# A long convolution by FFT stages, then soft MoE slots: the first stage in three products of column halves, with other stores and loads around it

## The chip, the cores and the metric

The kernel runs on one core of one Trainium2 chip. All data is float32. The metric is the device time of one execution in microseconds; before the change it is 932.87 us, the median of three runs (930.76 to 934.02). A core has a matrix engine (TensorE, PE in the profile; its weight loads are PEld), VectorE (DVE), ScalarE (ACT), GpSimd (POOL) and SyncE (SP), which here only issues DMAs. Sixteen DMA engines move data between the chip's memory (HBM) and the on-chip SBUF. TensorE writes to PSUM, and ScalarE or VectorE carry its results from there to SBUF; that is called an eviction.

## The reference

```python
def _attn_ref(x, h):                 # x: (8, 5696, 128), h: (5696, 128)
    L = 2 * S
    Xf = np.fft.rfft(x, n=L, axis=1)
    Hf = np.fft.rfft(h, n=L, axis=0)
    return np.fft.irfft(Xf * Hf[None], n=L, axis=1)[:, :S, :]

def _moe_ref(x, phi, w1, w2):        # x: the result above as (45568, 128); 32 slots, 8 experts
    logits = x @ phi
    d = softmax of logits over the tokens
    slot_input = d.T @ x
    slot_out[e] = np.maximum(slot_input[e] @ w1[e], 0) @ w2[e]
    c = softmax of logits over the slots
    return c @ slot_out
```

Each of the 8 sequences is convolved causally with h along its 5696 positions, channel by channel. The result goes through a soft mixture of experts: every token is weighed into 32 slots, the slots pass through small networks, and each token gets a mixture of the slots back.

## The kernel before, in words

**The transform.** A sequence is seen as a table of R1 = 89 rows by N2 = 64 columns (a position is row times 64 plus column), padded in theory to N1 = 90 rows. A transform over the rows gives 90 frequencies k1; for each of these a transform over the 64 columns follows. Columns n and 63 - n are folded first: their sum and their difference are transformed separately with cosines and sines of half the size. That makes these stages:

- *Stage A* (`stage_a`, lines 204 to 219): for a chunk of CH = 4 columns of the lower half and the 4 mirrored ones, multiply the folded rows by a table over all 90 frequencies. For the sum (comp 0) the two products are the cosine table and the negative sine table; for the difference (comp 1) they are the negative sine table and the negative cosine table. Each product is one matmul of 128 rows by 128 table columns on 512 elements (4 columns of 128 channels). The 90 frequencies lie as two groups of 45 table columns, at F0 = 6 and F1 = 82. ScalarE evicts each product into a buffer `fst` (three of these), and two DMAs store it to a scratch tensor f in HBM, one for each group: 45 partitions, 4 columns, and runs of 1 KB (cosine and sine part of 128 channels). So a chunk costs four matmul products, four evictions and four stores of 180 KB.
- *Stage B1* (`stage_b1`): for two frequencies at a time (a "unit", 23 in a sequence), load f from HBM (`load_g`, line 230, tile gt, 256 KB in 128 partitions, 2 KB runs), transform over the columns, and multiply with the spectrum of h (Hr, Hi).
- *Stage B2* (`stage_b2`): the way back over the columns; evicted into `zst` (five buffers) and stored to a scratch tensor z in HBM (line 289, 256 KB, 1 KB runs).
- *Stages C1 to C6*: for two chunks at a time ("a pair T") load z (`load_pair`, line 319: 1024 KB and 416 KB, 16 KB runs), go back over the rows, unfold, transpose, and do the logits, both softmaxes and the sum into the slots, with a running maximum.

h is treated as sequence 0; its B1 makes Hr and Hi. After the last tokens the experts are computed and every token's output is made and stored.

**Loading x.** `load_x` (lines 178 to 191) fetches one chunk: for each of 89 rows, two runs of 2 KB, the lower columns and the mirrored ones. It does so in two DMAs, of 80 and of 9 rows, to partitions 20 to 108 of one of three buffers `xc`. The other partitions hold zeros, and so do those rows of the table. `fold` (lines 195 to 202) makes the sum or the difference on GpSimd, each into its own single buffer, `x0` or `x1`, of [128, 512].

**The order of the work.** The order is written out by hand: a loop over steps t (line 557), one chunk a step, with the stages of earlier data woven in at fixed lags (LAG_B = 9 steps, LAG_C = 27). Every engine takes its instructions in this order, and SyncE issues all loads and stores in this order too, one after the other; an issue whose buffer isn't free, or whose data isn't there, holds up all that follow. A step has about three units of B in its `slot_b` calls; each first loads gt for a unit four units ahead, unless that unit belongs to a new sequence whose f isn't complete. Every second step has the work of a pair (C1, C4, C5), the others its transposes and sums (C2, C3, dispatch).

In a step before the change the order is: stage A on the sum, with its stores; the fold of the next chunk's sum; dispatch; slot_b; C1, C4, C2, C6; slot_b; the load of a pair; the load of chunk t + 3; the additions of C1; C5; stage A on the difference, with its stores; the fold of the next difference; C3; slot_b; the rest of the softmaxes.

Steps 0 to 71 have stage A; after that the same loop goes on without it, until the last units are through.

Of the kernel before, what the change touches and what calls it, by code (L numbers as in the profile page):

```python
# [10 lines left out]
F32 = mybir.dt.float32  # L11
AF = mybir.ActivationFunctionType
# [10 lines left out]
def transform_tables(S, N1, N2, CH, X0, F0, F1):  # L23
# [21 lines left out]
    part = s1  # L45
    s1 = np.zeros((P, 3, P))
    for a, p in enumerate((F0, F1)):
        s1[X0:X0 + R1, :, p:p + NP] = part[:, :, a * NP:(a + 1) * NP]
# [26 lines left out]
def kernel(  # L75
# [42 lines left out]
    SPLIT = R1 // 16 * 16  # L118
    X0, F0, F1 = 20, 6, 82
# [4 lines left out]
        for n, t in zip(("s1", "i1", "w", "v", "turn"), transform_tables(S, N1, N2, CH, X0, F0, F1))]  # L124
# [35 lines left out]
    s1 = apool.tile([P, 3, P], F32, name="s1", tag="s1", bufs=1)  # L160
# [13 lines left out]
    xcs = [apool.tile([P, 2, CH, D], F32, name=f"xc{i}", tag=f"xc{i}", bufs=1) for i in range(3)]  # L174
# [3 lines left out]
    def load_x(c):  # L178
        if c >= (B + 1) * NJ:
            return  # L180
        g, j = divmod(c, NJ)
        src = (h if g == 0 else x[g - 1]).rearrange("(a n) d -> a n d", n=N2)
        t_ = xcs[c % len(xcs)]
        gap = N2 - CH * (2 * j + 1)
        for r in (slice(0, SPLIT), slice(SPLIT, R1)):
            v = src[r, CH * j:CH * (j + 1), :]
            v = bass.AP(tensor=v.tensor, offset=v.offset,
                        ap=[v.ap[0], [gap * D, 2], [1, CH * D]])
            nc.sync.dma_start(
                out=t_[X0 + r.start:X0 + r.stop, :, :, :].rearrange("p s n d -> p s (n d)"), in_=v)  # L190
        xs[c] = t_
# [3 lines left out]
    def fold(c, comp):  # L195
        if c not in xs:
            return
        t_ = xs.pop(c) if comp else xs[c]
        y_ = xf[comp]
        nc.gpsimd.tensor_tensor(out=y_[:, :, :], in0=t_[:, 0, :, :], in1=t_[:, 1, ::-1, :],  # L200
                                op=AL.subtract if comp else AL.add)
        folded[(c, comp)] = y_

    def stage_a(c, comp):
        g, j = divmod(c, NJ)
        src = folded.pop((c, comp))
        tab = (0, 1) if comp == 0 else (1, 2)
        st = apool.tile([P, CH, 2, D], F32, name="fst", tag="fst", bufs=3)
        for G in range(2):
            p = bank()  # L210
            nc.tensor.matmul(p[:, :], s1[:, tab[G], :],  # L211
                             src[:, :, :].rearrange("p n d -> p (n d)"), start=True, stop=True)
            nc.scalar.activation(st[:, :, G, :],  # L213
                                 p[:, :].rearrange("p (n d) -> p n d", d=D), AF.Copy)
        n0 = comp * HALF + CH * j
        for a, p in enumerate((F0, F1)):
            nc.sync.dma_start(
                out=fd[g][a, n0:n0 + CH, :, :, :].rearrange("n q c d -> q n (c d)"),
                in_=st[p:p + NP, :, :, :].rearrange("k n c d -> k n (c d)"))
# [54 lines left out]
    def stage_b2(u):  # L274
# [12 lines left out]
        st = bpool.tile([P, 2, 2 * D], F32, name="zst", tag="zst", bufs=5)  # L287
# [257 lines left out]
    nc.scalar.dma_start(out=s1[:, :, :], in_=t_s1)  # L545
    for c in range(1, 3):
        load_x(c)
# [9 lines left out]
    for t in range(last_front + 1):  # L557
# [83 lines left out]
        stage_a(t, 0)  # L641
        fold(t + 1, 0)
        if t == NA - 1:
            stage_a(t, 1)
        if pair(3) is not None:
            dispatch(pair(3))
        slot_b()
        T, U = pair(0), pair(2)
# [11 lines left out]
        slot_b()  # L660
        if pair(-2) is not None:
            load_pair(pair(-2))
        load_x(t + 3)
# [6 lines left out]
        if t < NA - 1:  # L670
            stage_a(t, 1)
            fold(t + 1, 1)
# [236 lines left out]
```

## Time and profile before

| | us | share of the span |
|---|---|---|
| span of the profiled run | 933.3 | |
| PE busy | 842.3 | 90% |
| DVE busy | 664.2 | 71% |
| ACT busy | 511.5 | 55% |
| POOL busy | 469.6 | 50% |
| L211, stage A's matmuls (576 instructions) | 284.3 | |
| L213, their evictions (288, 597 ns each) | 167.7 | |
| L200, the folds (144, 1277 ns each) | 183.7 | |
| L336, C1's matmuls in column halves (448 instructions) | 112.9 | |

A float32 matmul product appears as two instructions, so the 288 products of stage A are 576 entries. The DMA queue moves 273.04 MB in 172,239 packets, 293 GB/s on average.

A page of the profile gives each engine's busy time, and then its course over the span in 40 slices, where a digit 9 means 90% or more. A busy PE isn't PE at its peak, since matmuls are pipelined and their ends are modelled. The DMA share is the mean over sixteen engines, so it can hide that some carry less than others. In the waits, "A <- B" means that A sat idle until B let it go; for SyncE's queue, "SPq", an issue stood still.

The run falls into parts: up to some 100 us stage A and the spectrum of h, up to some 225 us stages A and B, from there to 690 us all stages together, and then the last sequence's B and C, the experts, and from about 850 us the output.

### The profile page before, as it was taken

What the parts mean: (1) busy time and instruction counts of PE and PEld (TensorE: products, weight loads), DVE (VectorE), ACT (ScalarE), POOL (GpSimd) and SP (SyncE); (2) the same over time, 40 slices, a digit from 0 to 9 for tenths busy, and PEclk for the clock granted to TensorE, in tenths of its full rate; (3) what the DMA queues carried; (4) which work ended last, traced back from release to release, by engine and by line L of the source; (5) the groups of instructions that cost most, each with busy time, mean ns of one, the idle gap of its engine ahead of it and who ended that gap; (6) DMA issues with size and microseconds to landing.
All of it is one profiled execution on the core that took longest, in us unless ns stands there. A gap on an engine that the chain in (4) does not pass through costs nothing. (4 is left out here: it accounts for less than half of the span.)

```text
span 933.3 us, 20359 instructions
## 1 busy us (share of the span) xinstructions
PE 842.3 (90%) x7220; PEld 402.3 (43%) x7220; DVE 664.2 (71%) x1127; ACT 511.5 (55%) x1016; POOL 469.6 (50%) x431
## 2 busy tenths in 40 slices
PE   6978788899999999999999999989998888996893
PEld 2323233334444444444444444434443434453793
DVE  3035576678878877888888788858878886795542
ACT  3556544455656655666666566646664444574442
POOL 4647623245555555555555555545545665468000
PEclk9989999999999999999999999989999988998956
DMA  9999899999999989999999999989979886675798
GB/s 296 272 270 277 264 325 316 295 306 318 284 296 311 332 262 298 321 328 279 291 308 333 280 310 309 308 270 307 319 258 279 288 269 230 218 273 196 272 405 327
DMA packets 172239, 273.04 MB, mean 293 GB/s; under 512 B 14742, under 2 KB 117398, under 8 KB 168965
## 3 DMA queue, kind: packets, MB, share of 16 engines
q1 hardware_dynamic: 171563, 271.38, 90.9%
q8 instruction: 58, 0.95, 0.4%
q10 hardware_dynamic: 576, 0.36, 0.2%
q14 instruction: 42, 0.34, 0.1%
HBM read 142.85 MB, written 128.21 MB: 290 GB/s over the span
## 5 line engine op out<-in xcount | busy, mean ns | idle before, releaser
L211 PE MATMUL bank<-x,s 128*128 128x512 f32 x576 | 284.3, 621 | 9.9 <-POOL x L200 8.0
L200 POOL TENSOR_TENSOR x<-xc 128x512 f32<-128x512 f32 x144 | 183.7, 1277 | 144.9 <-PE bank L211 90.8
L213 ACT ACTIVATE fst<-bank 128x512 f32<-128x512 f32 x288 | 167.7, 597 | 91.7 <-PE bank L211 63.6
L265 DVE TENSOR_TENSOR pr<-bt,Hr 128x512 f32<-128x512 f32 (+1 forms) x184 | 126.6, 688 | 100.1 <-PE bt L244 97.1
L288 ACT ACTIVATE zst<-bz 128x512 f32<-128x512 f32 (+1 forms) x184 | 108.2, 588 | 153.7 <-PE bz L284 147.8
L244 PE MATMUL bt<-gt,wt 64*64 64x256 f32 x1620 | 140.1, 409 | 45.8 <-DMA gt<-f 16.1
L211 PEld LDWEIGHTS bank<-x,s 128*128 128x128 f32 x576 | 100.1, 192 | 133.2 <-issue 88.8
L270 DVE TENSOR_TENSOR yf<-pr,pi 128x512 f32<-128x512 f32 (+1 forms) x169 | 145.2, 859 | 5.8
L268 DVE TENSOR_TENSOR pi<-bt,Hi 128x512 f32<-128x512 f32 (+1 forms) x184 | 125.0, 679 | 0.0
L284 PE MATMUL bz<-yf,vt 64*64 64x256 f32 x1440 | 118.7, 389 | 2.2 <-ACT yt L371 0.5
L244 PEld LDWEIGHTS bt<-gt,wt 64*64 64x64 f32 x1620 | 45.4, 133 | 163.1 <-PE bank L211 45.3
L336 PE MATMUL bank<-zc,i 128*64 128x512 f32 x448 | 112.9, 628 | 0.0
L359 POOL TENSOR_TENSOR y<-y,op 128x512 f32<-128x512 f32 x64 | 77.5, 1211 | 60.3 <-DVE op L341 57.7
L359 POOL TENSOR_TENSOR y<-y,om 128x512 f32<-128x512 f32 x54 | 75.9, 1405 | 2.1
L284 PEld LDWEIGHTS bz<-yf,vt 64*64 64x64 f32 x1440 | 53.2, 134 | 37.8 <-issue 12.8
L255 DVE SCALAR_TENSOR_TENSOR Hr<-bt,turn,ph 128x128 f32<-128x128 f32 (+1 forms) x46 | 16.0, 348 | 68.9 <-ACT ph L253 68.9
L371 ACT ACTIVATE yt<-bank 128x360 f32<-128x360 f32 x128 | 51.9, 472 | 15.8 <-PE bank L369 15.6
L369 PE MATMUL bank<-ident,y 109*128 109x109 f32 x512 | 58.9, 268 | 1.0 <-DVE y L359 0.7
L415 POOL MEMSET dt<- 64x8 f32 x32 | 3.4, 107 | 109.3 <-ACT dn L418 87.0
L369 PEld LDWEIGHTS bank<-ident,y 109*128 109x128 f32 x512 | 50.5, 145 | 16.6 <-issue 10.8
L860 PE MATMUL op<-so,cT 32*128 32x128 f32 x704 | 44.9, 376 | 6.2 <-ACT o L869 5.8
L336 PEld LDWEIGHTS bank<-zc,i 128*64 128x64 f32 x448 | 28.1, 140 | 51.4 <-issue 46.3
(100 smaller groups left out, 910.1 us busy)
## 6 DMA issues: line engine op xcount, KB each, us to landing
f<-fst SPq DMA_DIRECT2D x288, 180.0 KB
gt<-f SPq DMA_DIRECT2D x198, 256.0 KB
z<-zst SPq DMA_DIRECT2D x176, 256.0 KB
zc<-z SPq DMA_DIRECT2D x28, 1024.0 KB
xc<-in_x_dram SPq DMA_DIRECT2D x64, 320.0 KB
out_dram<-o SPq DMA_DIRECT2D x15, 1024.0 KB
zc<-z SPq DMA_DIRECT2D x28, 416.0 KB
out_dram<-o SPq DMA_DIRECT2D x9, 768.0 KB
```

The lines of the kernel that those rows point to most:

```text
L200: nc.gpsimd.tensor_tensor(out=y_[:, :, :], in0=t_[:, 0, :, :], in1=t_[:, 1, ::-1, :], op=AL.subtract if comp else AL.add)
L211: nc.tensor.matmul(p[:, :], s1[:, tab[G], :], src[:, :, :].rearrange("p n d -> p (n d)"), start=True, stop=True)
L213: nc.scalar.activation(st[:, :, G, :], p[:, :].rearrange("p (n d) -> p n d", d=D), AF.Copy)
L244: nc.tensor.matmul(bt[q * HP:(q + 1) * HP, a, 0:2 * D], wt[r, 2 * i + q, :], t_[r, q, :, :].rearrange("p c d -> p (c d)"), start=True, sto ...
L265: nc.vector.tensor_tensor(out=pr[r, :, :, :], in0=pv, in1=Hr[r, i, :, :].unsqueeze(2).broadcast_to([n * HP, 2, 2, D]), op=AL.mult)
L268: nc.vector.tensor_tensor(out=pi[r, :, :, :], in0=pv, in1=Hi[r, i, :, :, :], op=AL.mult)
L270: adder.tensor_tensor(out=y_[r, :, :, :], in0=pr[r, :, :, :], in1=pi[r, :, ::-1, :], op=AL.add)
L284: nc.tensor.matmul(bz[a * HP:(a + 1) * HP, q, 0:2 * D], vt[r, i, a, :], y_[r, a, :, :].rearrange("p c d -> p (c d)"), start=True, stop=True)
L288: nc.scalar.activation(st[:, 0:n, :], bz[:, 0:n, 0:2 * D], AF.Copy)
L336: nc.tensor.matmul(p[h_ * HP:(h_ + 1) * HP, :], i1[:, tab, :], t_[:, h_, o, :, q, :], start=True, stop=True)
L359: eng.tensor_tensor(out=part_, in0=part(v, 0), in1=o_[:, :, :], op=sign)
L369: nc.tensor.transpose(p[:, i * TR:(i + 1) * TR], ys[T][0:TR, k * CH + i, 0:D], ident[0:TR, 0:TR])
```

## The change

Four things change together.

1. *Three products.* Sum and difference of a chunk share one matmul product in PSUM: the sum's 64 table columns give partitions 0 to 63, the difference's give 64 to 127. A half holds at most 64 frequencies, so 60 of the 90 (NPAIR) are done with two such products, which give their two parts (tables 0 and 1 for the sum, 1 and 2 for the difference). The other 30 frequencies, both parts, make 60 columns: a third product ("late"), later in the step. So a chunk has three products and three evictions in place of four.
2. *Six stores.* The first two products are stored by four DMAs, of 45 and 15 partitions for the sum and for the difference, with 1 KB runs. In the late product both parts of a frequency lie in neighbouring partitions, so its two stores, of 60 partitions, have runs of 512 B. The stores are issued later than their evictions: the first four after the step's first slot_b, the late two after the loads of a pair and of x.
3. *x.* One load brings two chunks, with runs of 4 KB, in DMAs of 64, 24 and 1 rows, every second step, into one of two buffers. The sum goes to one of two buffers by turns, and the difference is written over the lower columns in place.
4. *zst* has four buffers in place of five; the x buffers take the room.

```diff
-        for r in (slice(0, SPLIT), slice(SPLIT, R1)):
-            v = src[r, CH * j:CH * (j + 1), :]
+        for r, n, p in x_blocks(R1):                # (0, 64, 32), (64, 24, 0), (88, 1, 24)
+            v = src[r:r + n, CH * j:CH * (j + 2), :]
             v = bass.AP(tensor=v.tensor, offset=v.offset,
-                        ap=[v.ap[0], [gap * D, 2], [1, CH * D]])
+                        ap=[v.ap[0], [(N2 - 2 * CH * (j + 1)) * D, 2], [1, 2 * CH * D]])
...
-        y_ = xf[comp]
+        y_ = lo if comp else xf[c % 2][:, :, :]
...
-        st = apool.tile([P, CH, 2, D], F32, name="fst", tag="fst", bufs=3)
-        for G in range(2):
+        if late:
+            st = apool.tile([P, CH, D], F32, name="fsr", tag="fsr")
+            dst = [(2, st[:, :, :])]
+        else:
+            st = apool.tile([P, CH, 2, D], F32, name="fst", tag="fst")
+            dst = [(G, st[:, :, G, :]) for G in range(2)]
+        for G, d_ in dst:
             p = bank()
-            nc.tensor.matmul(p[:, :], s1[:, tab[G], :], src..., start=True, stop=True)
-            nc.scalar.activation(st[:, :, G, :], p..., AF.Copy)
-        for a, p in enumerate((F0, F1)):
-            nc.sync.dma_start(
-                out=fd[g][a, n0:n0 + CH, :, :, :].rearrange("n q c d -> q n (c d)"),
-                in_=st[p:p + NP, :, :, :].rearrange("k n c d -> k n (c d)"))
+            for h_ in range(2):
+                nc.tensor.matmul(p[h_ * HP:(h_ + 1) * HP, :], s1[:, h_, G, :], src[h_],
+                                 start=True, stop=True)
+            nc.scalar.activation(d_, p[:, :].rearrange("p (n d) -> p n d", d=D), AF.Copy)
+        def store():
+            for h_ in range(2):
+                v = fd[g][:, h_ * HALF + CH * j:h_ * HALF + CH * (j + 1), :, :, :]
+                p0 = h_ * HP
+                if late:
+                    nc.sync.dma_start(
+                        out=v[1, :, NPAIR - NP:, :, :].rearrange("n q c d -> (q c) n d"),
+                        in_=st[p0:p0 + 2 * (N1 - NPAIR), :, :])
+                    continue
+                for a, q in ((0, NP), (1, NPAIR - NP)):
+                    nc.sync.dma_start(
+                        out=v[a, :, 0:q, :, :].rearrange("n q c d -> q n (c d)"),
+                        in_=st[p0 + a * NP:p0 + a * NP + q, :, :, :]...)
+        return store
...
-        st = bpool.tile([P, 2, 2 * D], F32, name="zst", tag="zst", bufs=5)
+        st = bpool.tile([P, 2, 2 * D], F32, name="zst", tag="zst", bufs=4)
...
-        stage_a(t, 0)
+        store = stage_a(t, False)
         fold(t + 1, 0)
...
         slot_b()
+        store()
...
         slot_b()
+        if t < NA - 1:
+            rest = stage_a(t, True)
+            fold(t + 1, 1)
         if pair(-2) is not None:
             load_pair(pair(-2))
-        load_x(t + 3)
+        if t % 2:
+            load_x(t + 3)
+        if t < NA - 1:
+            rest()
...
-        if t < NA - 1:
-            stage_a(t, 1)
-            fold(t + 1, 1)
```

## Prediction

> **What bounds the kernel now.** I read the page first (its 40 slices), then the table of stretches, the waits, the timeline of one pair of steps, and last the packet records grouped by size.
>
> ```profile
> span 933.3 us, 20359 instructions
> PE     6978788899999999999999999989998888996893
> DMA  9999899999999989999999999989979886675798
> q1 hardware_dynamic: 171563, 271.38, 90.9%
> ```
>
> TensorE and the DMA engines are both near full from slice 8 to slice 29; neither can be called the bound from the page alone. Slices of 25 us say more (columns: busy us of each engine with instruction counts, granted clock, DMA share, GB/s):
>
> ```profile
> 125.00:150.00 25.00, 21.61 (x168) 8.57 (x168) 17.81 (x28) 12.54 (x22) 7.66 (x6) 1.00 1.00 319
> 325.00:350.00 25.00, 22.75 (x190) 10.41 (x189) 18.50 (x33) 14.20 (x28) 14.03 (x12) 1.00 0.89 268
> 375.00:400.00 25.00, 25.00 (x212) 11.34 (x208) 21.81 (x36) 15.83 (x32) 12.89 (x12) 1.00 1.00 320
> 575.00:600.00 25.00, 25.00 (x212) 11.47 (x210) 21.83 (x36) 15.42 (x31) 12.79 (x11) 1.00 1.01 322
> 875.00:900.00 25.00, 21.12 (x298) 19.60 (x297) 12.47 (x21) 10.62 (x22) 0.00 (x0) 0.65 1.05 406
> ```
>
> Within a batch TensorE works all 25.00 us and the DMA share is 1.00 to 1.01. The last stretch, pure output stores, shows a full DMA system: 1.05 (packets overlap a little). At a batch's border (325 to 350) both drop. The timeline there:
>
> ```profile
> 344.78 1.98 PE L211 MATMUL bank<-x,s 128*128 128x512 f32 x4
> 349.02 0.66 PE L244 MATMUL bt<-gt,wt 64*64 64x256 f32 x8 [2.25 <-DMA gt<-f]
> ```
>
> The first load of a new batch's f waits until the old stores of f have landed. Who waits on the SyncE queue from 300 to 690 us:
>
> ```profile
> SPq L217 <- DMA zc<-z: 73.0, 29, 4.7
> SPq L230 <- DMA f<-fst: 13.6, 6, 4.1
> ```
>
> The first is a full queue (an issue waits for one some eight issues back), the second the border. TensorE waits for a gt only at borders. So TensorE is the bound inside a batch, DMA stands right behind it, and the border costs both.
>
> **How close is DMA?** 139 stores of f in 390 us, four to a step: 34.75 steps of 11.2 us. Of f, 45 partitions a store. The Trainium skill (DMA: Bandwidth & Descriptors, "Why a DMA increments its semaphore by 16 and not by 1") says that a DMA uses the largest number of engines up to 16 that divides its outermost dimension: 15 here, the sixteenth idle. The trace agrees: 14,486 packets of 4 bytes, and one per engine and DMA under that rule sums to about 14,430 (288 x 15 for f, 207 x 16 for gt, and so on). KB per step on engines 0 to 8: f 48, gt 45, z 45, zc 48, x 24, c 5.6, sum 215.6; mean of all sixteen 207.9. From 300 to 690 us the share is 0.97 on average, so the fullest engines stand at 0.97 x 215.6/207.9 = 1.006 of the possible 1.05: 96%, borders included. A batch of 8 steps (89.8 us) has 86.2 us of transfers on them and 3.6 us of holes, of which the border is about 25 us x 0.09 = 2.3.
>
> **Packet prices.** From the packet records of 300 to 690 us, mean (median): 1 KB 49 ns (46), 2 KB 109 (84), 4 KB 176 (159). The medians give 8 ns a packet and 37.5 ns a KB. The same page, "Why small descriptors are slow", says that each packet has a fixed overhead; the trace agrees with 8 ns. Its "Specifications" ask for 512 B or more for line rate; no 512 B packet is in this trace.
>
> **Part 1: three products of column halves.** Per step four full products become three, each as two halves of 64 columns. TensorEngine Tiling, "Key Properties": column tiles operate independently. The trace agrees:
>
> ```profile
> 455.46 1.98 PE L211 MATMUL bank<-x,s 128*128 128x512 f32 x4
> 457.38 0.81 PE L378 MATMUL bank<-yt,phi 128*32 128x360 f32 x8
> ...
> 462.31 1.94 PE L336 MATMUL bank<-zc,i 128*64 128x512 f32 x8
> 464.18 0.66 PE L407 MATMUL bank<-ident,lt 128*128 128x128 f32 x4
> ```
>
> Two full products take 1.92 us to the next instruction, two products in halves 1.87. So TensorE saves 4 x 0.96 - 3 x 0.935 = 1.03 us of 11.2 a step; over 72 steps 74 us of work. ScalarE saves one eviction of 597 ns; it wasn't the bound. Were DMA free, 43.7 steps between 200 and 690 us would give 45 us. DMA has only 4%.
>
> **Part 2: six stores of f.** Per engine and step, 48 packets of 1 KB become 32 of 1 KB and 32 of 512 B. Price of 512 B: low 27 ns (8 + 19), high 38 (between 33 for 368 B and 48 for 768 B, means of the table loads), I take 29 (27 plus the 1 KB packets' excess over their median). Then 32 x 49 + 32 x 29 - 48 x 49 = +144 ns (ends +80 and +432). All stores still use 15 engines. Two more completions: +18 ns. SyncE issues 6 instead of 4 stores at about 0.45 us, and 1.5 instead of 2 x loads: 14.7 DMAs a step, 6.6 us of 11.2, hidden.
>
> **Part 3: x in 4 KB runs.** Per engine and step 12 packets of 2 KB (1308 ns) become 6 of 4 KB; at 176 to 215 ns (the latter in the first 50 us) that is -252 to -18; I take -135. The lone row 89 falls on engines 0 and 1: half a packet a step, +98. Parts 2 and 3 together: +27 ns on most engines, +125 on two; I take 70/1.05 = 0.067 us, x 72 = +4.8 us.
>
> **Part 4: order at the border.** The load of a pair (1.44 MB) is followed by x and the old batch's last f, then z, then the waiting gt. Before, 2.16 MB stood up to the end of f and 616 KB (z and the next step's f) behind it, which kept DMA at work while gt waited. After, the next step's four stores come after slot_b, hence behind the waiting gt: 256 KB of cover. At 310 GB/s the hole grows by 1.2 us; eight borders, 0 to 9.6 us, I take half, +4.8, since other loads are ahead of their need by then.
>
> **Part 5: looser ties.** Folded sums alternate between two buffers and differences lie in place, so POOL no longer waits for TensorE (90.8 us of waits, off the bound); fst has 2 + 2 buffers for two steps instead of 3 for one and a half. In the first 200 us the DMA share is 0.89 to 1.00 with TensorE at 68 to 92%: better decoupling may give 2%, -4. Inside batches the 1.3 us of holes that aren't the border shrink to 0.4 when TensorE no longer holds buffers: -0.9 x 5.5 batches = -4.9. The x load now waits for TensorE's late product, and behind it stands only that product's own store, which waits longer: 0. Four z buffers: a buffer comes back after four units, 15 us, and even behind a pair load z lands within some 11: 0, up to 1 us a border. First load twice as large, both folds first: +1.2, partly under 2.9 MB of tables.
>
> Sum: +4.8 + 4.8 - 4 - 4.9 + 1.2 = +1.9: 934.8, say 934.
>
> **Rivals.** (a) DMA fills its holes: transfers take 86.7 of each 87.5 us, no larger border: -2.3 x 5.5 - 4 = -17 against 932.9: 916. For: the DMA queue is rarely empty, and TensorE, the bound today, reaches 25.00 of 25. Against: between 130 and 200 us TensorE is not the bound, and yet DMA shows the same 0.98. (b) 512 B costs 35 ns or so and the hole comes in full: 32 x 6 = +192 ns more a step, 13 us, and + 4.8, on 934: 952. For: stores are scattered at 45 KB steps. Against: 1 KB stores stay at 49, near their median.
>
> **Chances.** Forecast (DMA takes over, little is won) 0.45 at 934, itself spread by some 5 us; (a) 0.30; (b) 0.25, from 938 up. Faster by 0.3% (under 930.1): 0.28 of (a) + 0.10 = 0.38; slower (over 935.7): 0.22 + 0.15 = 0.37; same 0.25. Range: 912, a little below (a), to 948; about 1 in 10 is left out above, 1 in 10 below.
>
> **What would show it.** The new product line's busy time near 218 us (864 instructions at L336's 112.9/448 us) against 284 for L211; TensorE below 24 of 25 us within batches while DMA stays 1.00 or more, with "PE <- DMA gt" waits inside batches; 4 KB packets under 200 ns and 512 B near 29; step near 11.2 us; a longer gap at each border. Steps of 10.5 us with DMA over 320 GB/s would prove me wrong: then DMA had room that its share doesn't show. A step over 11.5 us with 512 B at 35 ns or more is case (b).

## The result and the profile after

The changed kernel takes 1034.97 us (median of 4, 1024.03 to 1037.73) against 933.44 us before (median of 4 on the same chip): a ratio of 1.1058, 95% interval 1.0965 to 1.1151. It is slower by a tenth, far outside the forecast range. Some executions are slow ones, over 1.5% above the fastest of the same kernel; the ratios of this document leave them out, the medians don't, and where that matters (run 5 most) the distance by the ratio stands beside.

The page of the changed kernel, the lines that answer to those read before:

```profile
span 1033.2 us, 20832 instructions
PE   5757678768888998989898989798989788896984
DMA  8886769999989999999999999999999897687598
q1 hardware_dynamic: 183866, 271.39, 87.1%
```

The row of TensorE is broken by 7s and 8s where it stood at 9; DMA is still near 9 later on, but shows 6, 7, 6 in slices 4 to 6. The bytes are the same (271.39 MB) in 12,303 more packets. Stretches of the changed kernel (columns as before), with the middle of the run, 300 to 680 us, as the last line:

```profile
125.00:150.00 25.00, 17.85 (x96) 4.99 (x92) 10.44 (x23) 8.90 (x18) 12.45 (x12) 0.80 0.64 177
325.00:350.00 25.00, 21.38 (x178) 7.73 (x180) 16.88 (x26) 10.96 (x21) 10.10 (x10) 0.86 0.93 279
375.00:400.00 25.00, 23.75 (x250) 10.38 (x250) 22.53 (x35) 14.36 (x28) 15.22 (x14) 1.00 0.96 288
300.00:680.00 380.00, 335.36 (x3009) 140.29 (x3002) 289.76 (x460) 192.01 (x377) 195.03 (x169) 0.95 0.94 272
```

The same middle in the kernel before:

```profile
300.00:680.00 380.00, 372.69 (x3161) 172.21 (x3156) 312.00 (x507) 229.15 (x445) 210.59 (x182) 0.99 0.97 304
```

Two different losses stand here. At 125 to 150 us both TensorE and DMA stand idle for much of the time (17.85 us busy of 25 against 21.61; a DMA share of 0.64 and 177 GB/s against 1.00 and 319): something else holds them. In the middle the DMA share hardly falls, from 0.97 to 0.94, yet it moves 272 GB/s where it moved 304: a busy share is not a rate.

Where the 99.9 us lie, by the start of the first eviction of each step, in us:

| | first eviction | steps 0-7 | 8-15 | 16-23 | 24-31 | 32-39 | 40-47 | 48-55 | 56-63 | 64-70 | step 71 to the end |
|---|---|---|---|---|---|---|---|---|---|---|---|
| before | 10.1 | 33.4 | 57.1 | 63.7 | 81.6 | 89.7 | 92.3 | 89.2 | 89.4 | 82.5 | 244.1 |
| changed | 13.5 | 37.7 | 78.3 | 72.6 | 95.4 | 100.3 | 98.6 | 102.2 | 99.2 | 87.3 | 248.0 |

The first 24 steps lose 34 us, of which 21 in steps 8 to 15 alone; steps 24 to 70 lose 58, some 10 a batch; the start and the end lose 3.4 and 3.9.

**Inside a batch: loads of f come late.** Groups of TensorE instructions of the changed kernel:

```profile
L233 PE MATMUL bank<-xc,s 128*64 128x512 f32 x432 | 226.3, 641 | 18.3 <-POOL xc L214 18.3
L233 PE MATMUL bank<-x,s 128*64 128x512 f32 x432 | 225.0, 634 | 18.8 <-POOL x L214 18.7
L276 PE MATMUL bt<-gt,wt 64*64 64x256 f32 x1620 | 147.2, 431 | 113.4 <-DMA gt<-f 82.6 <-issue 10.2 <-PE bz L316 8.1
L368 PE MATMUL bank<-zc,i 128*64 128x512 f32 x448 | 129.5, 708 | 0.0
```

The last two of these in the kernel before:

```profile
L244 PE MATMUL bt<-gt,wt 64*64 64x256 f32 x1620 | 140.1, 409 | 45.8 <-DMA gt<-f 16.1 <-PE bz L284 10.7 <-issue 10.2
L336 PE MATMUL bank<-zc,i 128*64 128x512 f32 x448 | 112.9, 628 | 0.0
```

The first two rows are the halves of the same products and overlap; together L233 covers 240.3 us against 284.3 for L211, 44 us less. Two things take it back. The third row: idle time ahead of B's first product because a load of f hasn't landed was 16.1 us and is 82.6. The fourth: C1's products, which the change doesn't touch, took 708 ns each where they took 628. The records of the granted clock have TensorE at half of full speed for 197 us of the changed run and for 95 before (41 and 10 of them between 300 and 690 us), and an instruction of C1's then takes 1.06 us in the median in place of 0.59. So TensorE's busy time as a whole did not fall (843.6 us against 842.3). All nine half-clock stretches between 300 and 690 us begin in one of the holes listed below or at most 1.4 us behind it; no run separates the loss by the holes from that by the clock.

A piece of the timeline, TensorE of the changed kernel:

```profile
457.42 0.59 PE L233 MATMUL bank<-x,s 128*64 128x512 f32 x1
457.43 0.59 PE L233 MATMUL bank<-xc,s 128*64 128x512 f32 x1
462.02 1.13 PE L276 MATMUL bt<-gt,wt 64*64 64x256 f32 x8 [4.00 <-DMA gt<-f]
```

Such holes stand in the trace at 310.5, 334.9, 362.3, 387.7, 413.1, 436.7 and 462.0 us, and so on: 15 of over half a microsecond between 300 and 690 us, one for each two steps, 42.4 us in all. Before there were three (6.2 us), in the first steps of a batch (a batch is the 8 steps of one sequence). Two steps have one pair load and one x load. What SyncE issued ahead of that hole:

```profile
448.28 1.18 SPq L351 DMA_DIRECT2D zc<-z  x2
449.57 1.60 SPq L199 DMA_DIRECT2D xc<-in_x_dram  x3
451.26 0.95 SPq L242 DMA_DIRECT2D f<-fsr  x2
452.26 0.48 SPq L262 DMA_DIRECT2D gt<-f  x1
456.35 0.39 SPq L321 DMA_DIRECT2D z<-zst  x1
458.40 0.33 SPq L262 DMA_DIRECT2D gt<-f  x1
```

The gt issued at 452.26 is the one that TensorE takes at 462.02 (the n-th load belongs to the n-th unit). It comes 9.8 us after its issue: in front of it stand 1440 KB of z, 712 KB of x and 240 KB of f. From 448.28 to 462.02 these and its own 256 KB make 2.71 MB in 13.7 us, 198 GB/s. The Trainium skill (DMA: Bandwidth & Descriptors, "Queues, rings and completion order") says that each DMA engine takes the descriptors of a queue in ring order; the trace agrees: this load waits its turn for 9.8 us. The kernel before, at the same place:

```profile
447.51 1.12 SPq L319 DMA_DIRECT2D zc<-z  x2
448.68 1.04 SPq L189 DMA_DIRECT2D xc<-in_x_dram  x2
449.82 1.60 SPq L217 DMA_DIRECT2D f<-fst  x2
451.52 0.45 SPq L230 DMA_DIRECT2D gt<-f  x1
```

```profile
461.29 0.66 PE L244 MATMUL bt<-gt,wt 64*64 64x256 f32 x8 [0.16 <-DMA gt<-f]
```

This load too came 9.8 us after its issue, but TensorE had stood idle for it for only 0.16 us. So the long wait behind a pair load isn't new, and the kernel before had little time to spare there. What differs in this pair is when TensorE wants the data: 9.6 us after the issue before, 5.8 us after it now. Over all pair loads between 300 and 690 us the first gt behind one took 8.3 us from issue to landing before and 9.5 now, and TensorE was ready for it 9.7 us after the issue before and 7.3 now (medians, 17 and 16 loads). The load got longer by a little, and the lead (the time from the issue to TensorE being ready) shorter by twice as much.

Count back from the z store, which SyncE could issue only at 456.35: gt, two fsr, three xc, two zc, eight in all, and the eighth is the first zc. The records say why. The DMAs take eight semaphores by turns, 133 or 134 DMAs each on SyncE's queue, and an issue waits until the DMA that had its semaphore last has landed (1,045 of SyncE's 1,066 issues do). So at most eight are under way; the number comes from the program's semaphores, and no run changes it. The queue stands still until the pair load has landed:

```profile
SPq L321 <- DMA zc<-z: 44.7, 12, 4.6
SPq L262 <- DMA zc<-z: 39.4, 18, 4.4
```

Before, this wait fell on L217, a store of f, and what stood behind it waited too. Now it falls on L262, the load that TensorE needs, and on L321, a z store with such a load behind it.

The packets of x got slow as well (records of 300 to 680 us): 4 KB 265 ns on average and 266 in the median (forecast 176 to 215), 8 KB, where two runs are joined, 558. Packets of 512 B took 32 ns (median 27).

**In the h part: a loop over GpSimd.** The waits of the changed kernel from 75 to 150 us:

```profile
POOL Hi L293 <- DVE Hi L290: 31.5, 13, 4.7
...
PEld bank L233 <- POOL xc L214: 22.0, 7, 4.5
...
PE bank L233 <- POOL xc L214: 15.8, 7, 3.7
```

The first was 8.6 us before, and TensorE waited 0.2 us for a fold in these 75:

```profile
POOL Hi L261 <- DVE Hi L258: 8.6, 14, 0.9
```

GpSimd's timeline of the changed kernel:

```profile
114.31 0.85 POOL L293 TENSOR_SCALAR Hi<-Hi 128x256 f32<-128x256 f32 x1 [4.34 <-DVE Hi L290]
116.03 0.85 POOL L293 TENSOR_SCALAR Hi<-Hi 128x256 f32<-128x256 f32 x1 [0.88 <-DVE Hi L290]
116.85 1.26 POOL L214 TENSOR_TENSOR xc<-xc 128x512 f32<-128x512 f32 x1
118.10 0.85 POOL L293 TENSOR_SCALAR Hi<-Hi 128x256 f32<-128x256 f32 x1
```

A product in column halves needs sum and difference at its start. The fold of the difference (L214, xc<-xc) stands behind two sign changes of the spectrum (L293) in GpSimd's order, these wait for VectorE, which waits for ScalarE (39.8 us in these 75) and TensorE's B1 of the same step. TensorE's next step waits for the fold: a loop through four engines, some 10 us a step (steps 8 to 15 take 78.3 us), where before the difference was needed only late in the next step.

### The profile page after: what moved, and what is told of

It reads as the page before. It is cut to its first block, busy times and chain, and to the rows that moved or that the text cites. A ratio compares the mean times of both kernels' runs of the same rounds, so it can differ in the third digit from the quotient of the medians.

```text
span 1033.2 us, 20832 instructions
## 1 busy us (share of the span) xinstructions
PE 843.6 (82%) x7508; PEld 369.4 (36%) x7508; DVE 677.7 (66%) x1126; ACT 474.6 (46%) x944; POOL 468.9 (45%) x431
## 3 DMA queue, kind: packets, MB, share of 16 engines
q1 hardware_dynamic: 183866, 271.39, 87.1%
## 5 line engine op out<-in xcount | busy, mean ns | idle before, releaser
L233 PE MATMUL bank<-xc,s 128*64 128x512 f32 x432 | 226.3, 641 | 18.3 <-POOL xc L214 18.3
L233 PE MATMUL bank<-x,s 128*64 128x512 f32 x432 | 225.0, 634 | 18.8 <-POOL x L214 18.7
L276 PE MATMUL bt<-gt,wt 64*64 64x256 f32 x1620 | 147.2, 431 | 113.4 <-DMA gt<-f 82.6
L214 POOL TENSOR_TENSOR x<-xc 128x512 f32<-128x512 f32 x72 | 101.4, 1408 | 196.7 <-DMA xc<-in_x_dram 119.9
L302 DVE TENSOR_TENSOR yf<-pr,pi 128x512 f32<-128x512 f32 (+1 forms) x169 | 163.3, 967 | 5.8
L316 PE MATMUL bz<-yf,vt 64*64 64x256 f32 x1440 | 126.4, 412 | 8.2 <-ACT lt L413 3.5
L368 PE MATMUL bank<-zc,i 128*64 128x512 f32 x448 | 129.5, 708 | 0.0
L235 ACT ACTIVATE fst<-bank 128x512 f32<-128x512 f32 x144 | 85.8, 597 | 78.7 <-PE bank L233 58.4
L214 POOL TENSOR_TENSOR xc<-xc 128x512 f32<-128x512 f32 x72 | 91.7, 1273 | 3.4
L233 PEld LDWEIGHTS bank<-x,s 128*64 128x64 f32 x432 | 49.3, 140 | 106.9 <-issue 79.9
L233 PEld LDWEIGHTS bank<-xc,s 128*64 128x64 f32 x432 | 50.4, 141 | 45.8 <-POOL xc L214 30.3
```

The source lines that it names most:

```text
L214: nc.gpsimd.tensor_tensor(out=y_, in0=lo, in1=up, op=AL.subtract if comp else AL.add)
L233: nc.tensor.matmul(p[h_ * HP:(h_ + 1) * HP, :], s1[:, h_, G, :], src[h_], start=True, stop=True)
L235: nc.scalar.activation(d_, p[:, :].rearrange("p (n d) -> p n d", d=D), AF.Copy)
L276: nc.tensor.matmul(bt[q * HP:(q + 1) * HP, a, 0:2 * D], wt[r, 2 * i + q, :], t_[r, q, :, :].rearrange("p c d -> p (c d)"), start=True, sto ...
L302: adder.tensor_tensor(out=y_[r, :, :, :], in0=pr[r, :, :, :], in1=pi[r, :, ::-1, :], op=AL.add)
L316: nc.tensor.matmul(bz[a * HP:(a + 1) * HP, q, 0:2 * D], vt[r, i, a, :], y_[r, a, :, :].rearrange("p c d -> p (c d)"), start=True, stop=True)
```

## The experiments

Times are medians. "+" is the distance from the median of the kernel before in the same session (931.1 to 934.5), the ratio stands with its 95% interval, and "by the ratio" is the distance that the ratio gives. The changed kernel is at +101.5 on this scale.

**1. Six stores with the packets of before.** The kernel before, the store of the upper group cut in two.

```diff
-            nc.sync.dma_start(out=fd[g][a, n0:n0 + CH, :, :, :]..., in_=st[p:p + NP, ...])
+            for q0, q1 in ((0, NP),) if a == 0 else ((0, 30), (30, NP)):
+                nc.sync.dma_start(out=fd[g][a, n0:n0 + CH, q0:q1, :, :]..., in_=st[p + q0:p + q1, ...])
```

> The kernel before with one of its four f stores a step pair of groups cut in two (30 and 15 partitions), so six stores a step with the same bytes, the same 1 KB packets and the same engines as before. Theory Q (the number of DMAs on SyncE's queue, eight of them in flight at a time, sets the pace: before and after both issue 1.16 to 1.17 DMAs per us between 300 and 690 us): 13.2 DMAs a step become 15.2, so 8 to 13% slower, 1005 to 1055 us. Theory P (packet prices on the DMA engines): only completions are added, within 1%, 930 to 942 us. Theory H (order on POOL) expects no change.

Measured: 966.25 us, +34.5; ratio 1.0407 (1.032 to 1.0494). Between the two expectations. Same bytes, same packets, 144 DMAs more: 0.24 us for each. The first gt behind a pair load took 8.1 us, no longer than before, but TensorE was ready for it 7.4 us after its issue (9.7 before). The wait for the pair load moves in part off the stores of f:

```profile
SPq L290 <- DMA zc<-z: 44.7, 12, 4.9
SPq L218 <- DMA zc<-z: 32.7, 19, 3.9
```

**2. Two tiny stores.** The kernel before, with two DMAs of one 512 B row a step to a scratch tensor that nobody reads.

```diff
+        nc.sync.dma_start(out=pad[2 * c + comp:2 * c + comp + 1, :], in_=ident[0:1, :])
```

> The kernel before with two more DMAs a step that move 512 B each, from one partition to a scratch row in HBM, right behind the f stores; everything else as before. They take a place in the queue and among the eight in flight, but next to nothing of the DMA engines. Theory Q (places in the queue): nearly the whole loss of the six stores (4.1%), so 955 to 970 us. If that loss came from the engines (each of the added stores starts and completes on 15 of them): within 1%, 925 to 940 us.

Measured: 952.16 us, +21.1; ratio 1.0214 (1.0136 to 1.0292). Just under the first expectation's range. 144 DMAs that move 74 KB in all cost 0.15 us each. They take a place among the eight. SyncE's own time is not short on the whole (between 300 and 690 us it stood idle for 0.31 of the time before in gaps of over 150 ns, and for 0.30 in this run), but between a pair load and the next gt it issues without a pause, and one more DMA there puts the gt back by 0.6 us (3.3 to 3.9 us in the median). The runs don't separate place and issue time. The waits of this run:

```profile
SPq L291 <- DMA zc<-z: 49.4, 13, 4.5
SPq L218 <- DMA zc<-z: 38.8, 20, 4.1
```

L291, the z store, again takes the wait that L217 had before.

**3. Late stores issued by ScalarE.** The changed kernel, in the late branch:

```diff
-                    nc.sync.dma_start(
+                    nc.scalar.dma_start(
```

> The changed kernel with the two late stores a step issued by ScalarE's queue in place of SyncE's. Packets, bytes and engines are those of the changed kernel. Theory Q in the form that SyncE's issue time is what counts: 12.7 DMAs a step are left on SyncE, 970 to 1000 us. In the form that the eight in flight count (they are shared by both queues): no gain, 1020 to 1045. Theory P: no change, 1025 to 1040 us.

Measured: 1107.88 us, +176.1; ratio 1.1884 (1.18 to 1.1969). Worse by another 75 us, beyond all three expectations. The Trainium skill (same page, "Issuing engines are not separate DMA queues") says that DMAs from several engines share the sixteen DMA engines and that a second issuer only saves issue time. The runs agree that nothing is won, and show a price. Both queues take their turns at the same eight semaphores, so SyncE now waits for the late stores of ScalarE to land. From 300 to 690 us of that run:

```profile
SPq L262 <- DMA f<-fsr: 81.3, 17, 6.9
SPq L321 <- DMA zc<-z: 35.9, 10, 6.3
```

```profile
PE bt L276 <- DMA gt<-f: 62.0, 18, 7.3
PEld bt L276 <- issue: 54.6, 36, 8.1
```

L262 is the load gt, and most of its wait is now for a store (81.3 us) and not for the pair load (39.4 in the changed kernel). ScalarE itself hardly waits at its issues, 4.6 us in 58 of them. The lead of the first gt behind a pair load falls to 5.3 us.

**4. Early fold.** The changed kernel, the difference folded right behind the sum:

```diff
         fold(t + 1, 0)
+        fold(t + 1, 1)
...
-            fold(t + 1, 1)
```

> The changed kernel with the fold of the next difference right after the fold of the next sum, ahead of GpSimd's sign changes of the step in the h part. Theory H: the part in which h's spectrum is made (steps 8 to 16, 78.3 us against 57.1 before) loses its waits of PE for POOL and gets 12 to 20 us shorter, all else the same: 1013 to 1023 us. The theories Q and P put that loss on the loads and stores: 1030 to 1040 us.

Measured: 1002.20 us, +70.4; ratio 1.0762 (1.0678 to 1.0847). 31 us come back, more than the expectation had. Steps 8 to 15 take 57.4 us in place of 78.3 (before: 57.1), and the stretch at 125 us has

```profile
125.00:150.00 25.00, 18.30 (x164) 5.83 (x164) 17.98 (x25) 10.15 (x17) 5.94 (x5) 1.00 0.94 282
```

282 GB/s in place of 177. The loop over GpSimd is the loss of the h part; the batches later keep theirs (99.5 to 101.9 us each between steps 32 and 63).

**5. The x part alone.** The kernel before with x in 4 KB runs, two chunks every second step behind the pair load, four z buffers.

```diff
+    return [(0, 64, 32), (64, 24, 0), (88, n - 88, 24)]
...
-        load_x(t + 3)
+        if t % 2:
+            load_x(t + 3)
```

> The kernel before with the x part of the change alone: two chunks in one load, runs of 4 KB, blocks of 64, 24 and 1 rows at the partitions of the change, two buffers, and four z buffers. Both folds go to buffers as before. Theory Q: 12.7 DMAs a step in place of 13.2: 2 to 4% faster, 895 to 920 us. Theory P (4 KB packets of x took 265 ns where two of 2 KB took 218, 24 rows on 12 engines into few partitions): 1 to 3% slower, 940 to 960 us.

Measured: 970.54 us, +38.7; ratio 1.0348 (1.0252 to 1.0443), by the ratio +32. Above both expectations. 4 KB packets: 273 ns.

**6. The same with the old row blocks.**

```diff
-    return [(0, 64, 32), (64, 24, 0), (88, n - 88, 24)]
+    return [(0, 80, 20), (80, n - 80, 100)]
```

> The x part alone as run before (two chunks a load, 4 KB runs, two buffers, four z buffers), but with the rows in the blocks of the kernel before: 80 rows at partitions 20 to 99 and 9 rows at 100 to 108. Theory of the places (the 24 rows in partitions 0 to 23 on 12 engines and the lone row on one or two hold up the load): most of the 3.5% comes back, 4 KB packets under 220 ns where they had 273, 925 to 945 us. Theory of the burst (twice as much x at once, behind the load of a pair): 955 to 975 us as with the new blocks.

Measured: 969.31 us, +38.2; ratio 1.0394 (1.0313 to 1.0474). The lone row, priced at +98 ns on two engines, isn't to be seen. The first gt behind a pair load took 11.1 us here, 9.3 in run 5 and 8.3 before, while TensorE was ready for it 10.1, 9.5 and 9.7 us after its issue: the burst lengthens the load, where the added stores shorten the lead. The same edit on the changed kernel with the early fold says the same:

> The changed kernel with the early fold of the difference and x in the blocks of 80 and 9 rows at partitions 20 to 108. With early fold alone it took 1002 us. Theory of the places: another 25 to 35 us less, 965 to 980; what is left over the kernel before is then the six stores. Theory of the burst: 995 to 1008.

Measured: 1005.97 us, +74.9; ratio 1.081 (1.0739 to 1.0881), beside +70.4.

**7. Four z buffers alone.** The kernel before with

```diff
-        st = bpool.tile([P, 2, 2 * D], F32, name="zst", tag="zst", bufs=5)
+        st = bpool.tile([P, 2, 2 * D], F32, name="zst", tag="zst", bufs=4)
```

> The kernel before with four z buffers in place of five, nothing else. My prediction put this at 0 to 1 us: 928 to 938. If the buffers are what holds ScalarE and with it the eight in flight, up to the whole loss of the x part: 950 to 970.

Measured: 932.41 us, +1.3; ratio 1.0001 (0.9972 to 1.0031): nothing, as forecast.

**8. Two chunks at once in 2 KB runs.** The kernel before, four x buffers, four z buffers:

```diff
-        load_x(t + 3)
+        if t % 2:
+            load_x(t + 3)
+            load_x(t + 4)
```

> The kernel before with the loads of two chunks issued together every second step, but each as before: 2 KB runs, 80 and 9 rows, so four x DMAs in two steps as before (four one-chunk buffers, four z buffers). Theory R (the 4 KB runs are what costs, 273 to 313 ns a packet): no change, 928 to 940 us. Theory B (712 KB of x at once, right behind the 1.44 MB of a pair): most of the 3.5 to 3.9% of the x part, 958 to 972.

Measured: 967.54 us, +35.7; ratio 1.0411 (1.032 to 1.0501). No longer run, no other packet, the same loss: it isn't the size of the runs. The loss comes another way, though: with four x DMAs behind the pair load the next gt itself has to wait for a place, and is issued 8.7 us after the pair load (3.3 before), so that its lead is 4.1 us.

**9. 4 KB runs without the burst.** The kernel before, one side (356 KB) a step at the step's end:

```diff
-        load_x(t + 3)
...
         slot_b()
+        load_x(t + 3 if t % 2 else t + 4, t % 2)
```

> The kernel before with x in 4 KB runs over two chunks, but the lower columns loaded in one step and the mirrored ones in the next, so 356 KB a step in two DMAs of 80 and 9 rows as before, at the step's end (two buffers, four z buffers). Theory R: the 3.5 to 3.9% of the x part, 955 to 972 us, 4 KB packets near 270 to 310 ns. Theory B: no change, 928 to 942, packets below 230.

Measured: 925.58 us, -6.3; ratio 0.9943 (0.9916 to 0.9969), by the ratio -5: under both expectations, and a little faster than before. 4 KB packets 190 ns.

**10. The burst in another place.** Run 5 with the same 712 KB at the end of even steps, which have no pair load:

```diff
-        if t % 2:
-            load_x(t + 3)
...
         slot_b()
+        if t % 2 == 0:
+            load_x(t + 4)
```

> The kernel before with the x load of two chunks in 4 KB runs and four z buffers, as in the run of the x part alone (970.5 us), but the 712 KB of x are issued at the end of the even steps, which load no pair, and not right behind the pair load of the odd steps. If the burst costs because it stands behind the pair load and in front of the loads of f that TensorE waits for, the time falls to 930 to 945 us. If a load of 712 KB at once costs wherever it stands, it stays at 960 to 972 us.

Measured: 936.53 us, +4.0; ratio 1.0052 (1.002 to 1.0083), by the ratio +5. Only the place differs from run 5, and by the ratios 28 of 32 us are gone. In the new place x is also asked for some half a step sooner, but lateness of x was not what run 5 paid for: TensorE's weight loads waited 4.6 us for a fold between 300 and 680 us there, and 5.0 before. The middle of run 5 and then of this run:

```profile
300.00:680.00 380.00, 358.76 (x3025) 165.79 (x3017) 296.41 (x480) 217.58 (x424) 203.75 (x175) 0.98 0.94 287
```

```profile
300.00:680.00 380.00, 373.25 (x3207) 173.68 (x3205) 313.98 (x510) 231.67 (x450) 216.22 (x185) 1.00 0.95 302
```

TensorE is back at 373 of 380 us, and its holes for a gt between 300 and 690 us fall from 8 (18.1 us) to 3 (6.1 us). The packets changed too: 4 KB of x from 273 ns on average (281 in the median) to 230 (159), 8 KB from 507 (522) to 466 (334). The same rows at the same distance are read; so it is what else is under way that slows them.

**11. Three products with the old x loads.** The changed kernel with the early fold, 80 and 9 rows, 2 KB runs, one chunk a step in three buffers, still behind the pair load.

```diff
-        t_ = xcs[c // 2 % 2]
+        t_ = xcs[c % 3]
...
-            v = src[r:r + n, CH * j:CH * (j + 2), :]
+            v = src[r:r + n, CH * j:CH * (j + 1), :]
...
-        if t % 2:
-            load_x(t + 3)
+        load_x(t + 3)
```

> The changed kernel with the early fold and with x loaded as before (one chunk a load, 2 KB runs, 80 and 9 rows, three buffers); three products, six stores with 512 B runs and their late issue stay. If the parts add up (six stores 34 us, x 36, late fold 33, and 74 us less TensorE work worth nothing): 960 to 972 us. If TensorE's relief is worth something once x is out of the way: 935 to 955. If 512 B or the late issue cost more than the number of stores: 975 to 1000.

Measured: 979.64 us, +47.8; ratio 1.0555 (1.0475 to 1.0636). Against the early fold with the old blocks (+74.9) the burst gives back 27. What is left of the change is three products, six stores and their order, and it stands 13 us over the six stores of run 1, with as many DMAs. Three runs each take one thing out of this one. The late stores in 1 KB packets from 30 partitions:

```diff
-                        out=v[1, :, NPAIR - NP:, :, :].rearrange("n q c d -> (q c) n d"),
-                        in_=st[p0:p0 + 2 * (N1 - NPAIR), :, :])
+                        out=v[1, :, NPAIR - NP:, :, :].rearrange("n q c d -> q n (c d)"),
+                        in_=st[p0:p0 + N1 - NPAIR, :, :, :].rearrange("k n c d -> k n (c d)"))
```

> The run with three products and the old x loads (979.6 us), with the two late stores of a step from 30 partitions in runs of 1 KB in place of 60 partitions in runs of 512 B: the same bytes and the same number of DMAs, half the packets (half of the frequencies' late values are zeros, so f's values are not those of the kernel before). If the packets of 512 B are what that run costs over six stores alone (966 us), 964 to 970 us. If it is the late order of the stores, or folds in place, it stays at 976 to 983 us.

Measured: 975.56 us, +43.1; ratio 1.0456 (1.0372 to 1.0539). Differences in buffers of their own, in the fold:

```diff
-        y_ = lo if comp else xf[c % 2][:, :, :]
+        y_ = xf[2 * comp + c % 2][:, :, :]
```

> The run with three products and the old x loads (979.6 us), with the differences in two buffers of their own, by turns, in place of over the lower columns of x. An x buffer then comes free with the fold, a step earlier, and the x load need not wait for TensorE's late product. If what that run costs over six stores alone (966 us) is this wait, which also holds up all DMAs queued behind the x load, 964 to 971 us; the waits of POOL's fold for x fall from 59 us to under 20. If it is the late order of the stores, 976 to 983 us.

Measured: 981.11 us, +46.6; ratio 1.0481 (1.0443 to 1.052). GpSimd's waits for x stay (57.4 us between 300 and 680, 59.3 in run 11), so the late release of the buffer wasn't their cause. Every store right behind its evictions:

```diff
-        store = stage_a(t, False)
+        stage_a(t, False)()
...
-            rest = stage_a(t, True)
+            stage_a(t, True)()
         if pair(-2) is not None:
             load_pair(pair(-2))
```

> The run with three products and the old x loads (979.6 us), with every store of f issued right behind its evictions: the four of the sum's and difference's products ahead of the first slot of B, the two late ones ahead of the pair load. If the late order of the stores costs what that run has over six stores alone (966 us), 964 to 971 us. If it is the x load that waits for the late product, 976 to 983 us, and possibly more, since the stores now hold up the loads of f behind them until their products are made.

Measured: 985.15 us, +50.7; ratio 1.054 (1.048 to 1.0599). None of the three brings it to run 1. Half the packets of the late stores (in that run half of their values are zeros) give 5 us, within the intervals. The 13 us are not settled: the intervals of run 1 and run 11 overlap by a fifth of a per cent. What the traces show is that TensorE's products wait for gt (300 to 680 us) for 34 us in run 11 (L275) and 15 in run 1 (L245), so that the work that three products save doesn't arrive in the time.

**12. All but the burst and the late fold.** The changed kernel with the early fold, 80 and 9 rows, 4 KB runs, the lower side at the end of odd steps, the mirrored one in the middle of even steps.

```diff
+        if t % 2 == 0 and t:
+            load_x(t + 2, 1)
...
         slot_b()
+        if t % 2:
+            load_x(t + 3, 0)
```

> The changed kernel with the fold of the difference right behind that of the sum, and x (still 4 KB runs, two buffers, difference in place) loaded one side a step: the lower columns at the end of odd steps, the mirrored ones in even steps behind the second slot of B. What is left of the change is three products, six stores and their late order. If late fold (33 us) and burst (36 us) are two costs that add up, and six stores cost what they cost alone, 1035 - 33 - 36 = 966 us, within 958 to 974. If the late order of the stores or the packets of 512 B cost something of their own, as the run with three products and the old x loads (979.6 us) suggests, 975 to 988 us.

Measured: 991.66 us, +59.2; ratio 1.0642 (1.0531 to 1.0754). Neither number of the expectation: the edit made a wait of its own. From 300 to 680 us:

```profile
POOL x L214 <- DMA xc<-in_x_dram: 101.7, 9, 12.2
...
PEld bank L462 <- POOL dt L447: 50.9, 15, 5.5
...
PE bank L462 <- POOL dt L447: 37.7, 15, 4.6
```

The mirrored side is asked for half a step before its fold; GpSimd stands up to 12.2 us, and TensorE behind it for the softmax work that GpSimd does next. Steps 0 to 7 take 48.8 us (37.9 with the early fold alone). The wait for gt, though, is off the list. As a test of whether the three costs add up this run decides nothing.

**13. One x load of 96 rows.** The kernel before, one DMA from partitions 20 to 115 for seven of the eight sequences, the rest as it was. The seven rows more meet rows of zeros in the table.

```diff
-        for r in (slice(0, SPLIT), slice(SPLIT, R1)):
+        for r in (slice(0, 96),) if one else (slice(0, SPLIT), slice(SPLIT, R1)):
```

> The kernel before with one x DMA a chunk in place of two for seven of the eight sequences: 96 rows at partitions 20 to 115 (the seven rows too many are the next sequence's and meet zero rows of the table, so the result is the same), on 16 engines. 8% more x bytes, one DMA a step less. Theory Q (a place in the queue costs some 10 us for 72, as the tiny stores did): 918 to 928 us, faster than before. If places in the queue only cost where they are added in a bad spot: 930 to 940.

Measured: 924.54 us, -7.3; ratio 0.9955 (0.9922 to 0.9989). By the ratio -4, so 56 DMAs fewer give 0.07 to 0.13 us each, though more bytes are moved.

**14. Runs 9 and 13 together.**

> The kernel before with the two edits that made it faster put together: x in 4 KB runs, one side a step at the step's end (925.6 us), and one DMA of 96 rows in place of 80 and 9 for seven of the eight sequences (924.5 us). The seven rows more that it loads meet rows of zeros in the table. If each gain is a cost of its own (packets of x, places in the DMA queue), they add: 933.4 - 7.9 - 8.9 = 917 us, within 914 to 921. If both give the same thing, DMA time around the x load, 922 to 927 us.

Measured: 922.29 us, -10.2; ratio 0.9898 (0.9825 to 0.997). The best of all here, faster than both kernels, but in the expectation's second range: the two gains do not add. Its page:

```profile
span 921.5 us, 20226 instructions
PE   5888888889999999999999999999998888996893
DMA  8989899999999999999999999989989887775798
```

TensorE stands at 9 from slice 10 to slice 30.

## Why the prediction was wrong

**What bounds the kernel: half right.** TensorE was at 25.00 of 25 inside batches and DMA close behind. But I measured DMA's room by the share of busy engines (96%), and there is a second limit that the share doesn't show: eight DMAs under way, and their order. "TensorE waits for a gt only at borders" was right to some 0.4 us, and hid that the gt behind a pair load came barely in time (8.3 us after its issue in the median, wanted after 9.7): I looked at the wait and not at the time to spare. The wait "SPq L217 <- DMA zc<-z" was quoted and called "a full queue (an issue waits for one some eight issues back)"; I didn't ask who would stand there after the change.

**Part 1: direction right, size off, and worth nothing.** The products take 240.3 us, not 218; their busy time falls by 0.61 us a step in place of 1.03. The 218 was scaled from C1's products at the clock of before. Now 27 us of the 240 lie in half-clock stretches; at full clock they would be about 14 us less (an estimate: half of 27), so the clock is some two thirds of the miss. The sign of the whole was right: it doesn't arrive in the time, but comes back in the waits for gt and in slower products.

**Part 2: the step that failed first.** "SyncE issues ... 6.6 us of 11.2, hidden" priced two more DMAs a step by issue time and 18 ns of completions. The 512 B packets were priced well (29, measured 32). The DMAs themselves cost 0.15 us each when empty and 0.24 with data moved into them: 34.5 us by run 1, where I had written nothing. What they delay is the issue of gt: the lead falls from 9.7 to 7.4 us (run 1).

**Part 3: the step that failed second.** -135 ns per engine and step on the ground of 4 KB at 176 to 215 ns. That price holds where x comes one side a step (190 ns, run 9, and then the kernel is faster), not behind a pair load (265 to 273). I priced the packets and not the place: 712 KB between the pair load and the gt that TensorE needs next. Runs 5, 6 and 8 put 32 to 38 us on it alone by their ratios, run 10 takes 28 of them back, and it is 27 inside the changed kernel. The lone row's +98 ns isn't to be seen.

**Part 4: not tested by itself.** With gt late in every pair of steps, the border has no clear share.

**Part 5: failed third, with the sign reversed.** "POOL no longer waits for TensorE": the wait of the folds for TensorE did fall (from 90.8 to 34.2 us), but both folds are now needed at the start of a step, and the fold of the difference stands behind the sign changes. Where I had put -4 for the first 200 us, the first 24 steps lost 34, and the early fold brings 31 us back, most of it there. The holes inside batches, which were to shrink (-4.9), grew: from 6.2 to 42.4 us of waits for gt between 300 and 690 us. The start was +3.4, not +1.2. Four z buffers at nothing was right.

**The rivals.** (b) came closest and for a reason that isn't the true one: it asked for 512 B at 35 ns and a step over 11.5 us; the step is 12.5 (a batch of 100.1 us) at 32 ns. Of the signs listed, waits for gt inside batches came, with TensorE below 24 of 25; DMA at 1.00 or more did not, and that was the sign that neither engine's speed had been the matter.

**The sum.** +101.5 = 31 for the late fold (run 4) + 27 for the burst (run 11 against the early fold with old blocks) + 34.5 for six stores (run 1) + 9 that stay open; four z buffers (run 7) are nothing, and the blocks of rows nothing that the intervals show. That the parts add up this way is bookkeeping over different runs; the one run meant to show it made a new wait.

## What to carry to other kernels

Ask of each added DMA which place it takes: who waits behind a long load for a free semaphore (in this program, eight issues behind), and what stands between that load and the next data that the busiest engine needs. Read two times off the trace for that data, from issue to landing and from issue to use: where they are nearly equal, as here before the change, there is no time to spare. Price a transfer by where it is issued, not by its packets alone: the same 712 KB cost 32 us or 5 by the ratios, and the longer runs gain when they are spread over the steps. Merging two products that took their operands at different times makes the later operand's producer, and all that is ahead of it on its engine, part of the next step's start.

## What the runs showed that I had not expected

A DMA costs 0.07 to 0.24 us in this kernel apart from its bytes: two tiny ones a step +21.1 us, two cuts a step +34.5, one of two merged -7.3 (by the ratio -4). Of the fifteen holes in TensorE's work between 300 and 690 us the seven over 3 us all had a half-clock stretch of 3.4 or 6.8 us at them, of the eight shorter ones two. A second issuing engine gave no more DMAs under way, since both take their turns at the same eight semaphores. Under a burst behind a pair load, DMA engines are 0.94 busy at 287 GB/s; with the burst elsewhere, 0.95 busy at 302; packets of 4 KB took 281 ns in the median and 159. Why they take longer beside the load of z isn't settled: no run reads x beside other traffic of the same size. And a kernel with three products but no more DMAs than before wasn't tried.
